# Six blocks of idle F32R matmuls of 192 and 384 columns behind the last product of a convolution and feed-forward kernel

## The chip, the cores and the metric

The kernel runs on one core of one Trainium2 chip. Its time is device microseconds of one execution, here the median of three runs. A separate execution was taken with the hardware profiler; its trace is what is read below.

## The reference

```python
def _attn_ref(x, weight):                      # x: 8 x 4096 x 192, weight: 8 heads x 7 taps
    w = softmax(weight, axis=-1)
    x_pad = np.concatenate([np.zeros((B, K - 1, D)), x], axis=1)
    x_unf = x_pad[:, idx, :].reshape(B, S, K, H, group)
    return np.einsum('hk,bskhg->bshg', w, x_unf).reshape(B, S, D)

def _moe_ref(x, w_in, w_out):                  # 32768 tokens, 192 -> 2048 -> 192
    h = x @ w_in
    g = np.where(h >= 1, h, np.where(h <= -1, 0.0, (h + 1) ** 2 / 4))
    return (g @ w_out).astype(np.float32)
```

The output of the first function, taken as 32768 tokens of 192 channels, is the input of the second. All is float32.

## The kernel before, in words

The tokens are worked off in 64 blocks of 512 (`TB`), the 2048 inner channels in eight pairs of 128 (`NPAIR`), so that the main loop has 512 steps `q`. Per step TensorE (PE) multiplies the tokens by a part of `w_in` (`mm1`, line 528) into the PSUM tile `h`, ScalarE and VectorE make `g` of it, and two or three steps later `mm2` (line 586) multiplies `g` by a part of `w_out` and adds into four PSUM tiles, `accm0`, `accm1`, `accr0` and `accr1`, until a block of tokens is done. To keep float32 accuracy with matmuls of the faster type F32R, the operands are split into a rounded part (`hi`) and the rest (`lo`), each of type F32R, and three of the four cross products are summed. The split `w_in` stays in SBUF for the whole kernel in eight tiles `W`, each of 128 partitions, two parts and 384 columns. The contraction length of 192 is 128 + 64 rows, so most matmuls take one half of PE's array (64 rows, `HALVES`), and two of them, one on each half, run as a pair. In the early steps plain F32 matmuls are used instead (lines 510, 513, 528, and 553 of `mm2_first`); one F32 product appears in the trace as two matmul instructions, each with a weight load of its own.

The order of the instructions is written out by hand (`manual_schedule`): each engine runs its own instructions in the order in which the program issues them, and waits for another engine only by semaphores.

The end is of its own. `evac_last` (lines 710 to 716) reads the four accumulators of the last block out to SBUF before the last pair of inner channels is added. `pair_last` then forms the last pair's product for each of four groups of 128 tokens in F32, 192 columns on the whole array (`units`, line 733), transposes the sums read out before (`others`, lines 737 and 738), adds both on VectorE (`total`, line 742) and stores the result (line 743). Groups 0 and 1 use tiles of `h`; groups 2 and 3 use new tiles with the names `accm0`, `accm1`, `accr0` and `accr1`. A new tile of such a name takes the place of the one before, and its first writer waits until the old one has been read.

At the start of the kernel the function `idle_matmuls` (line 786) issues seven bf16 matmuls whose results nothing reads.

Of the kernel before, what the change touches and what calls it, by code (L numbers as in the profile page):

```python
# [8 lines left out]
F32 = mybir.dt.float32  # L9
# [9 lines left out]
P = 128  # L19
TB = 512  # L20
# [13 lines left out]
def lightconv_then_ffn(ctx: ExitStack, tc: tile.TileContext, x, weight, w_in, w_out, out):  # L34
# [24 lines left out]
    nc = tc.nc  # L59
    B, S, D = x.shape  # L60
# [7 lines left out]
    NPAIR = NF // 2  # L68
# [3 lines left out]
    HALVES = (TOP, BOT)  # L72
# [10 lines left out]
    ps_o = ctx.enter_context(tc.tile_pool(name="ps_o", bufs=1, space=PSUM))  # L83
# [273 lines left out]
    W = [const.tile([P, 2, CI], F32R, name=f"w{j}") for j in range(NPAIR)]  # L357
# [177 lines left out]
    def tokens_of(t, b, turned):  # L535

        if not turned:
            return t[:, b * P:(b + 1) * P]
        return t.rearrange("p (k i a) -> p k a i", k=2, a=2)[:, b % 2, b // 2]
# [179 lines left out]
    def pair_last(q):  # L719

        s = q // NPAIR
        g, w = gs.pop(q), WF[NPAIR - 1 + LAG]
        y = [ob.tile([P, TB], F32, name="sum") for _ in range(2)]
        y = [y[b // 2][:, b % 2 * D:(b % 2 + 1) * D] for b in range(4)]
        h = [ps_h.tile([P, 2, TB], F32, name="h") for _ in range(2)]
        a = [ps_o.tile([P, TB], F32, name=n) for n in ("accm0", "accm1", "accr0", "accr1")]
        ps = [t[:, 0:D] for t in (h[0][:, 0], h[1][:, 0], a[0], a[1])]
        ot = [t[:, 0:D] for t in (h[0][:, 1], h[1][:, 1], a[2], a[3])]
        part = lambda a, b: last[a][:, b * P:(b + 1) * P]

        def units(b):
            for e in range(2):
                nc.tensor.matmul(ps[b], tokens_of(g[:, e], b, True), w[:, e, :],  # L733
                                 start=(e == 0), stop=(e == 1))

        def others(b):
            nc.tensor.matmul(ot[b][:, P:], part("r", b), ident[:, 0:DR], start=True, stop=True)  # L737
            nc.tensor.transpose(ot[b][:, 0:P], part("m", b), plain)
            nc.scalar.copy(y[b], ot[b])

        def total(b):
            nc.vector.tensor_tensor(out=y[b], in0=ps[b], in1=y[b], op=ALU.add)
            (nc.scalar if b == 2 else nc.sync).dma_start(
                out=out[s * TB + b * P:s * TB + (b + 1) * P], in_=y[b])

        units(0)
        units(1)
        others(0)
        others(1)
        total(0)  # L750
        total(1)
        units(2)
        others(2)
        others(3)
        units(3)
        total(2)
        total(3)


    whose = const.tile([P, 2 * P], F32, name="whose")  # L760
# [300 lines left out]
    for q in range(NQ + LATE):  # L1061
        s, j = divmod(q, NPAIR)
        c, i = divmod(q, 2 * NPAIR)
# [53 lines left out]
        else:  # L1117
# [12 lines left out]
            n = q - 1 if q < NF32 + 3 else q - 2  # L1130
# [66 lines left out]
```

## Time and profile before

| | |
|---|---|
| median of 3 runs | 2021.41 us (2021.04 to 2021.7) |
| the profiled execution | 2020.79 us |
| its span, first to last instruction | 2019.1 us |
| PE busy | 2014.9 us, 18659 matmuls |
| ScalarE, VectorE, GpSimd busy | 1955.8, 1873.3, 790.3 us |
| start of PE's last matmul, VectorE's last addition, the last store's issue | 2015.48, 2015.91, 2016.30 us |
| mean granted clock of PE | 1.000 |

Times inside the trace are microseconds from the start of the span. PE's matmuls are pipelined and the end of one is modelled, so the record of one is longer than the distance to the next one; what a matmul costs in a row of matmuls is read from the distances of their starts. PEld are the weight loads, which PE runs beside the matmuls. Line 1193 is the end of the program, where all engines meet.

### The profile page before, as it was taken

How to read it: one execution, taken by the hardware profiler on the slowest of the kernel's cores; microseconds unless marked ns; L12 is line 12 of the kernel's file. 1: busy time of each engine (PE TensorE's matmuls, PEld its weight loads, DVE VectorE, ACT ScalarE, POOL GpSimd, SP SyncE). 2: the span in 40 equal slices, each digit the busy share in tenths (PEclk: the TensorE clock that was granted, in tenths of full speed). 3: DMA queues.
4: the chain of work that ended last, by engine and by line, in shares of the span. 5: the costliest groups of instructions: out<-in, count | busy, mean ns of one | idle time of the engine just before them, and what ended most of it. 6: DMA issues, size and time to landing. Idle time of an engine off the chain costs nothing.

```text
span 2019.1 us, 46948 instructions
## 1 busy us (share of the span) xinstructions
PE 2014.9 (100%) x18659; PEld 1747.2 (87%) x18659; DVE 1873.3 (93%) x2109; ACT 1955.8 (97%) x2376; POOL 790.3 (39%) x762
## 2 busy tenths in 40 slices
PE   9999999999999999999999999999999999999999
PEld 7988888888888888888888888888888888888888
DVE  8899999999999999999999999999999999999988
ACT  8899999999999999999999999999999999999997
POOL 3534434343444343434433334344433343443340
PEclk9999999999999999999999999999999999999999
DMA  7334334443443434344434444344343434443332
GB/s 191 82 67 77 61 75 76 78 77 68 75 78 68 80 68 76 72 78 79 73 62 75 77 77 78 66 74 79 67 80 68 78 72 78 75 75 64 74 62 48
DMA packets 470909, 152.79 MB, mean 76 GB/s; under 512 B 419056, under 2 KB 426544, under 8 KB 470688
## 3 DMA queue, kind: packets, MB, share of 16 engines
q1 hardware_dynamic: 447008, 109.50, 26.9%
q0 software_dynamic: 23520, 40.19, 12.9%
q8 instruction: 146, 2.39, 0.5%
q14 instruction: 75, 0.61, 0.1%
q10 hardware_dynamic: 160, 0.10, 0.0%
HBM read 32.84 MB, written 25.17 MB: 29 GB/s over the span
## 4 chain that ended last, share of the span: by engine, by line
PE 100%; POOL 0%; DVE 0%; issue 0%; DVEq 0%
PE h L528 49%; PE accr L586 32%; PE accm L586 16%; PE accm L553 1%; PE accr L553 1%; PE accm L786 0%; PE accr L219 0%; PE accm L197 0%; PE h L733 0%; PE accm L733 0%; PE accr L513 0%; PE accr L510 0%; PE accm L510 0%; POOL t L778 0%; PE h L175 0%; PE h L737 0%
## 5 line engine op out<-in xcount | busy, mean ns | idle before, releaser
L639 DVE TENSOR_TENSOR gl<-g,gh 128x1024 fp32r<-128x1024 f32 x495 | 639.1, 1291 | 94.2 <-ACT gh L633 94.1
L968 DVE SCALAR_TENSOR_TENSOR g<-g,h 128x1024 f32<-128x1024 f32 (+1 forms) x506 | 608.8, 1203 | 9.4 <-ACT g L621 5.4
L528 PE MATMUL h<-hi,w 64*128 64x512 f32 x4048 | 602.1, 377 | 0.0
L586 PE MATMUL accr<-gh,wg 64*128 64x512 f32 x3960 | 587.6, 376 | 0.0
L621 ACT ACTIVATE g<-g 128x1024 f32<-128x1024 f32 x499 | 528.2, 1058 | 15.9
L620 ACT ACTIVATE g<-h 128x1024 f32<-128x1024 f32 x499 | 509.1, 1020 | 24.8 <-PE h L528 20.5
L633 ACT CAST gh<-g 128x1024 fp32r<-128x1024 f32 x495 | 513.8, 1038 | 1.2 <-DVE g L968 1.1
L528 PEld LDWEIGHTS h<-hi,w 64*128 64x128 f32 x4048 | 379.5, 186 | 56.5
L586 PEld LDWEIGHTS accr<-gh,wg 64*128 64x128 f32 x3960 | 370.8, 185 | 56.6
L270 POOL TENSOR_TENSOR y<-y,p 128x512 f32<-128x512 f32 x181 | 233.3, 1289 | 403.4 <-DVE m L645 289.3
L270 POOL TENSOR_TENSOR r<-r,p 128x512 f32<-128x512 f32 x180 | 231.6, 1287 | 402.1 <-DVE m L645 399.3
L528 PE MATMUL h<-lo,w 64*128 64x512 f32 x2024 | 382.2, 376 | 0.0
L586 PE MATMUL accr<-gl,words 64*128 64x512 f32 x1980 | 373.9, 376 | 0.0
L645 DVE TENSOR_TENSOR m<-gl 128x512 fp32r<-128x512 f32 x495 | 340.4, 688 | 27.2 <-DVE gl L639 0.9
L528 PE MATMUL h<-rh,w 64*128 64x512 f32 x1000 | 294.7, 376 | 0.0
L586 PE MATMUL accm<-gh,wg 64*128 64x512 f32 x1980 | 293.8, 376 | 0.0
L528 PE MATMUL h<-rhi,w 64*128 64x512 f32 x992 | 293.6, 376 | 0.0
L676 POOL DMA_DIRECT2D t<-t x244 | 206.8, 981 | 31.6 <-ACT t L666 23.2
L528 PEld LDWEIGHTS h<-lo,w 64*128 64x128 f32 x2024 | 189.9, 186 | 28.5
L586 PEld LDWEIGHTS accr<-gl,words 64*128 64x128 f32 x1980 | 185.8, 186 | 27.9
L586 PEld LDWEIGHTS accm<-gh,wg 64*128 64x128 f32 x1980 | 185.8, 186 | 27.9
L301 POOL TENSOR_TENSOR lo<-y,hi 128x512 fp32r<-128x512 f32 x62 | 79.9, 1289 | 316.5 <-ACT p L261 166.3
(170 smaller groups left out, 2379.6 us busy)
## 6 DMA issues: line engine op xcount, KB each, us to landing
t<-t POOLq DMA_DIRECT2D x183, 128.0 KB, 3.9
out_dram<-osb SPq DMA_DIRECT2D x366, 64.0 KB, 1.9
raw<-in_x_dram SPq DMA_DIRECT2D x334, 68.0 KB, 2.4
hi<-hi SPq DMA_DIRECT2D x130, 128.0 KB, 2.3
lo<-lo SPq DMA_DIRECT2D x128, 128.0 KB, 3.5
t<-t POOLq DMA_DIRECT2D x61, 256.0 KB, 3.2
rhi<-rh SPq DMA_DIRECT2D x62, 128.0 KB, 2.2
rlo<-rl SPq DMA_DIRECT2D x62, 128.0 KB, 3.5
```

The lines of the kernel that those rows point to most:

```text
L270: fresh.append(lambda p=self.product(k): nc.gpsimd.tensor_add(y, y, p))
L301: sub = eng.tensor_sub(lo, self.y, hi.bitcast(F32))
L528: nc.tensor.matmul(h[e], w[HALVES[e], c0:c0 + P], seen(x[e][e]), start=(n == 0), stop=(n == len(mms) - 1))
L553: nc.tensor.matmul(accs[s][a, i][:, c0:c0 + D], block, w[half, e, :], start=(j == 0 and e == 0 and b % 2 == 0), stop=(j == NPAIR - 1 and e ...
L586: mm = nc.tensor.matmul(accs[s][bank], w[half], in_turn(g[half]), start=(j == 0 and bank not in seen), stop=(j == NPAIR - 1 and k % 3 == 2 ...
L620: nc.scalar.activation(g[:, e, :], hs[q][:, e, :], AF.Relu, bias=0.5, scale=0.5)
L621: nc.scalar.activation(g[:, e, :], g[:, e, :], AF.Square)
L633: nc.scalar.copy(gh[:, e, :], gs[q][:, e, :])
L639: nc.vector.tensor_sub(gl[:, e, :], g[:, e, :], gh[:, e, :])
L645: return nc.vector.tensor_add(gt, gl[:, 0, :], gl[:, 1, :])
L676: nc.gpsimd.dma_start(out=to, in_=src, accum_op=ALU.add)
L968: nc.vector.scalar_tensor_tensor(out=g, in0=g, scalar=1.0, in1=h, op0=ALU.min, op1=ALU.max)
```

## The change

Behind the last call of `total`, `pair_last` calls a new function, `idle_blocks`. It takes four new PSUM tiles with the accumulators' names, of which it writes two, and issues six blocks of F32R matmuls. Weights and moving columns both come from the eight tiles `W` (both parts, 16 in all, one after another); `D` is 192, `P` is 128. Every matmul starts and ends its own sum, and nothing reads the results. In the sixth block the weights change only with every third matmul.

```diff
         total(2)
         total(3)
+        idle_blocks()
+
+    def idle_blocks():
+
+        t = [ps_o.tile([P, TB], F32, name=n) for n in ("accm0", "accm1", "accr0", "accr1")]
+        w = lambda i, n, half=slice(0, P): W[i % NPAIR][half, i // NPAIR % 2, 0:n]
+        for i in range(24):
+            nc.tensor.matmul(t[i % 2][:, 0:D], w(i, P), w(i + 11, D), start=True, stop=True)
+        for i in range(24):
+            for k, half in enumerate(HALVES):
+                nc.tensor.matmul(t[k][:, 0:D], w(i, P, half), w(i + 11, D, half),
+                                 start=True, stop=True)
+        for i in range(16):
+            nc.tensor.matmul(t[i % 2][:, 0:2 * D], w(i, P), w(i + 11, 2 * D),
+                             start=True, stop=True)
+        for i in range(16):
+            nc.tensor.matmul(t[i % 2][:, 0:D if i % 2 else 2 * D], w(i, P),
+                             w(i + 11, D if i % 2 else 2 * D), start=True, stop=True)
+        for i in range(16):
+            for k, half in enumerate(HALVES):
+                nc.tensor.matmul(t[k][:, 0:2 * D], w(i, P, half), w(i + 11, 2 * D, half),
+                                 start=True, stop=True)
+        for i in range(24):
+            nc.tensor.matmul(t[i % 2][:, 0:D], w(i // 3, P), w(i + 11, D), start=True, stop=True)
```

The order of PE's instructions changes at one place, its end. The first listing is the difference there: a row is a line, the operation, the tile written, the tiles read (the moving one first, then the weights) and the shape written; buffer numbers stand behind the names.

```order
 L733 MATMUL accm_30158<-wf_109,g_30079 128x192 x2
-L1193 UNCONDITIONAL_BRANCH
+L765 MATMUL accm_30189<-w_89,w_86 128x192
+L765 MATMUL accm_30190<-w_90,w_87 128x192
+L765 MATMUL accm_30189<-w_91,w_88 128x192
+L765 MATMUL accm_30190<-w_92,w_89 128x192
```

Where PE's program ended with the last product, the new matmuls follow; the branch to the end stands behind all 160 of them. The second listing is the same place of the changed kernel with full tile names and with what an instruction waits for.

```order
L738 MATMUL accr1_30160<-osb_29929,t_30139 128x128
L733 MATMUL accm1_30158<-wf9_109,g_30079 128x192 x2
L765 MATMUL accm0_30189<-w3_89,w0_86 128x192 [waits DVE_49]
L765 MATMUL accm1_30190<-w4_90,w1_87 128x192 [waits DVE_49]
L765 MATMUL accm0_30189<-w5_91,w2_88 128x192
L765 MATMUL accm1_30190<-w6_92,w3_89 128x192
```

Only the first two new matmuls wait, each for VectorE, which reads the `accm` tiles of the groups 2 and 3 before; no instruction of another engine is added, and none waits for the new matmuls but the program's end.

## Rows read from the trace of the kernel before

**Rows 1.** The page: its span, its part 1 for PE, its part 4.
```profile
span 2019.1 us, 46948 instructions
...
PE 2014.9 (100%) x18659; PEld 1747.2 (87%) x18659; DVE 1873.3 (93%) x2109; ACT 1955.8 (97%) x2376; POOL 790.3 (39%) x762
...
PE 100%; POOL 0%; DVE 0%; issue 0%; DVEq 0%
```

**Rows 2.** The time line from 2015 us: start, us, engine, line, instruction, count [idle before <-releaser].
```profile
2015.25 0.36 DVE L742 TENSOR_TENSOR sum<-accm,sum 128x192 f32<-128x192 f32 x1 [0.32 <-ACT sum L739]
...
2015.48 0.33 PE L733 MATMUL accm<-wf,g 128*128 128x192 f32 x1
...
2015.91 0.36 DVE L742 TENSOR_TENSOR sum<-accm,sum 128x192 f32<-128x192 f32 x1 [0.31 <-PE accm L733]
2016.30 0.33 SPq L743 DMA_DIRECT2D out_dram<-sum  x1
```

**Rows 3.** Line L1193, the end: count, shortest/median/longest in ns, first and last start.
```profile
L1193 POOLq EVENT_SEMAPHORE  x4: 17/17/17, 2018.3 to 2019.0; - x4
...
L1193 SPq DRAIN  x3: 7/7/7, 2018.2 to 2018.5; - x3
L1193 PEldq DRAIN  x2: 13/900/1788, 2014.1 to 2018.6; - x2
```

**Rows 4.** Stretches: busy us of PE, PEld, DVE, ACT, POOL, granted clock, DMA share, GB/s.
```profile
2015.80:2018.30 2.50, 0.01 (x1) 0.00 (x0) 0.36 (x1) 0.00 (x0) 0.00 (x0) 1.00 0.38 127
2018.30:2019.10 0.80, 0.00 (x0) 0.00 (x0) 0.00 (x0) 0.00 (x0) 0.00 (x0) 0.50 0.00 0
```

**Rows 5.** The time line from 2012.6 us: a read-out and the weight load behind it.
```profile
2012.66 0.37 ACT L716 COPY t<-accr 64x256 f32<-64x256 f32 x1 [0.50 <-DVE t L714]
2013.08 0.19 PEld L737 LDWEIGHTS h<-ident,t 128*128 128x128 f32 x1
```

**Rows 6.** The chain in order of time at 1005 us: start, us, what.
```profile
1005.54 1.94 PE h L528 x18
1007.48 0.65 PE accr L586 x6
```

**Rows 7.** The time line from 2013.2 us, L737 and L738.
```profile
2013.47 0.33 PE L737 MATMUL h<-ident,t 128*128 128x64 f32 x2
...
2013.53 0.20 PEld L738 LDWEIGHTS h<-osb,t 128*128 128x128 f32 x1
...
2013.64 0.28 PE L738 MATMUL h<-osb,t 128*128 128x128 f32 x1
```

**Rows 8.** The same time line, L733 and what follows it.
```profile
2013.64 0.65 PEld L733 LDWEIGHTS accm<-wf,g 128*128 128x128 f32 x4
2013.76 0.82 PE L733 MATMUL accm<-wf,g 128*128 128x192 f32 x4
...
2014.41 0.33 PE L737 MATMUL accr<-ident,t 128*128 128x64 f32 x2
```

**Rows 9.** The time line from 11.5 us, weight loads of L513 on the two halves.
```profile
11.71 0.18 PEld L513 LDWEIGHTS accr<-rh,p 64*128 64x128 f32 x1 [0.33 <-issue]
11.71 0.18 PEld L513 LDWEIGHTS accm<-rh,p 64*128 64x128 f32 x1
11.81 0.19 PEld L513 LDWEIGHTS accr<-rh,p 64*128 64x128 f32 x1
11.82 0.19 PEld L513 LDWEIGHTS accm<-rh,p 64*128 64x128 f32 x1
```

**Rows 10.** Groups by line, engine and shape: xcount | busy us, mean ns | idle before.
```profile
L786 PE MATMUL accm<-osb 128*128 128x512 bf16 x5 | 2.3, 629 | 0.0
```

**Rows 11.** The time line from 18 us, F32 matmuls of 192 columns on halves.
```profile
18.47 0.82 PE L553 MATMUL accr<-wf,g 64*128 64x192 f32 x8
...
19.12 0.82 PE L553 MATMUL accm<-wf,g 64*128 64x192 f32 x8
```

## The prediction

> **What bounds the kernel now.** I read the page first: TensorE (PE) is busy for the whole span of 2019.1 us and the chain that ended last is PE on nearly every step [rows 1]. So there is nothing ahead of the end to gain or lose; the change touches only what lies behind the last product. There the time line is the view to read [rows 2]. The last matmul of L733 starts at 2015.48 and its record ends at 2015.81; VectorE's last addition (L742) follows at 2015.91 for 0.36, SyncE issues the last store at 2016.30, and then no engine computes any more. The rows of line L1193, the program's end, show what closes it [rows 3]: PE's own drain begins at 2014.1, lasts 1.788 and so ends at 2015.9, just behind the last matmul. SyncE, which waits for the store, gets to its drain at 2018.2 to 2018.3, and from there a round of semaphores over all engines runs to 2019.1. PE is one of those that must arrive. From 2015.8 to 2018.3 it could therefore work for nothing, 2.5 us; each microsecond past 2018.3 is paid in full. The granted clock is 1.00 (2.4 GHz) up to 2018.3 and 0.50 behind it [rows 4]: PE had then been idle for 2.5 us. In the changed kernel PE resumes within 0.6 us, so I count everything at 2.4 GHz.
>
> **The change part by part.** It removes and moves nothing. It adds 160 matmuls (24 + 48 + 16 + 16 + 32 + 24), each with a weight load, in 120 slots (a pair on the halves is one), on PE alone, behind PE's last product: block 1, 24 on the whole array with 192 columns; block 2, 24 pairs on the halves with 192; block 3, 16 whole with 384; block 4, 16 whole that alternate 384 and 192; block 5, 16 pairs on the halves with 384; block 6, 24 whole with 192 where three in a row load the same weights. No other engine gets an instruction, no DMA is added, and nothing reads the results.
>
> *When it starts.* The first matmul writes accm0, which L742 has read by 2015.25 + 0.36 = 2015.61; it runs while PE would wait anyway and is not counted. The second writes accm1, which the last L742 reads until 2015.91 + 0.36 = 2016.27. From an engine's end to PE's load I take 0.05: L716 ended at 2012.66 + 0.37 = 2013.03 and the load that waited for it started at 2013.08 [rows 5]. A load with nothing to hide it takes 0.11 (below). So the second matmul runs from 2016.27 + 0.05 + 0.11 = 2016.43. SyncE's store was issued without PE and lies beside all this, hidden.
>
> *What a column costs.* All steady matmuls here are of the same type as the added ones (F32R), on halves, with 512 columns: 18 of them, nine pairs, in 1.94 us [rows 6], 0.2156 per pair, which is one column per cycle. The two halves of a pair run together. Scaled by columns, 384 cost 0.162 and 192 cost 0.081. For 384 this is nearly certain.
>
> *What a short matmul costs* is the open price: no row of the trace shows an F32R matmul below 512 columns, nor one on the whole array. Its load is fetched while the matmul before runs, so a slot is the longer of moving time and load time. From below: 0.081, the moving time alone, if the load is as short as that of the second pass of L737, which started 0.06 after the first, its load included (the pair begins at 2013.47, and the load of L738, which is issued as the second pass begins, at 2013.53) [rows 7]. Nearest to it: the load of L738 began at 2013.53 and its matmul at 2013.64, 0.11 later, although the matmul before it has only 64 columns. L738 is, like an added matmul, one instruction with one load of 128 columns of 4-byte weights; L737 is an F32 product in two passes with a load each. So I take **0.110 per 192-column slot**, bound by its load. From above: F32 products of 192 columns on the whole array (L733), four passes from 2013.76 to 2014.41 [rows 8]: 0.1625 a pass, two passes or 0.325 a product. For a pair on the halves I take the same 0.110: at L513 the loads of both halves were issued at 11.71 and the next two at 11.81 and 11.82 [rows 9], so they load side by side in 0.11. Repeated weights I count as loaded again, since every matmul of the trace has its own load.
>
> *The sum.* Block 1: 24 x 0.110 = 2.64. Block 2: 24 x 0.110 = 2.64. Block 3: 16 x 0.162 = 2.59. Block 4: eight times 0.162 (a 384, which hides the next load) + 0.110 = 2.18. Block 5: 2.59. Block 6: 2.64. Together 15.28, less the first matmul 15.17. Between whole array and halves there are four changes (blocks 1 to 2, 2 to 3, 4 to 5, 5 to 6). No row shows such a change without a wait in it; each costs nothing at least, and at most an emptied array: 0.17 by which the record of an L733 matmul (0.33) outlasts its slot, and 0.11 for an uncovered load, together 0.28. I take half, 0.14 each, 0.56.
>
> End: 2016.43 + 15.17 + 0.56 = 2032.16; the last record's tail 0.17, the drain some 0.05, the round of semaphores 2019.1 - 2018.3 = 0.8, and the span ends at 2033.18. That is 14.1 more than 2019.1. The profiled execution took 2020.79; with 14.1 it is 2034.9. It stands 0.6 below the median of the runs (2021.41), so I name **2035.5**.
>
> The Trainium skill ("TensorEngine Tiling (Array Packing)", Key Properties) says that changing the tiling mode drains TensorE. By that the changes would stand at the upper end, 1.12 in place of 0.56, and the time at 2036.1; no run here shows it yet.
>
> **The rivals.**
> *One column per cycle everywhere.* If the load hides even under 192 columns, block 1, 2 and 6 cost 1.94 each and block 4 costs 1.94: 12.95 in all, 2.3 less, **2033.2**. For it: the short loads of L737's second passes. Against it: L738.
> *Short F32R runs like F32.* If a matmul of 192 columns gets the F32 price of L733, 0.325, blocks 1, 2 and 6 cost 7.80 each and block 4 8 x (0.162 + 0.325) = 3.90: 32.48, 17.0 more, **2052.5**. For it: the fast pace is shown at 512 columns only, and operands are 4-byte in both. Against it: it is one instruction, F32 is two. Half of this (one pass at two cycles per column, 0.1625) gives 19.48 and **2039.6**.
> *Loads in line with matmuls.* If on the whole array the next load waits for the matmul to end, a 192 costs 0.081 + 0.110 = 0.191 and a 384 0.272: 4.58 + 2.64 + 4.35 + 3.70 + 2.59 + 4.58 = 22.44, 7.1 more, **2042.6**. Against it: L733's four loads stand inside its matmuls (from 2013.64 and 2013.76), with 0.1625 a slot, the time of the moving columns alone [rows 8]. The Trainium skill ("TensorE: Matmul & The Clock Gate", Part 3, The mechanism) says that a load overlaps running matmuls only if its row group differs, which would be this case; the trace disagrees with its 0.1625.
> *Not slower.* The matmuls don't reach the chip, or cost so little that they end before 2018.3: nothing reads their results, and a build may drop such work. The point that decides: 120 slots would have to fit into 2018.3 - 2016.43, 16 ns each, or be gone. Then **2021.4**. Against it: the idle matmuls of L786 are never read either and stand in the trace [rows 10], and the added ones stand in PE's order.
> *Fed too slowly.* On the halves, 192 columns in 0.110 ask for four instructions in that time, 27 ns each. At L553 sixteen instructions (eight matmuls, eight loads) take 0.65, 41 ns each [rows 11]; if that were PE's limit, block 2 would cost 24 x 0.163 = 3.90, 1.3 more: 2036.8.
>
> **How the numbers follow.** My forecast 0.37; one column per cycle everywhere 0.21; like F32 0.25; half of that 0.08; loads in line 0.04; not slower 0.02; 0.03 for the slow feeding and what I don't name. The forecast's own range is 2034.6 to 2036.8. The low end of the range is the rival at 0.081 without the 0.56 for the changes, 2032.6, and 0.3 for the spread of the runs; leaving out the F32 pace would leave out over 2 in 10, so the high end is that case with 1.12 for the changes, 2053.1. A measurement of this kernel can tell 0.2%, 4 us; every case but one is slower by over 10 us: slower 0.97, same 0.02, faster 0.01.
>
> **What would show it.** In the profile after: nothing changed up to 2015.8; PE resumes at about 2016.4; blocks 1 and 6 equal at 2.6 each, block 3 and 5 equal at 2.6, block 2 like block 1; granted clock 1.00 until PE's end; the span ends 0.8 to 0.9 behind PE. Block 1 at 1.9 shows the hidden load, at 3.9 or 7.8 a slower moving pace; block 6 shorter than block 1 shows that repeated weights cost less. A start later than 2016.5, or a clock of 0.50 inside the blocks, makes the sum wrong elsewhere.

## The result and the profile after

The changed kernel took 2036.11 us, median of 3 runs (2035.91 to 2036.52), against 2021.41 before: a ratio of 1.0073 with a 95% interval of 1.005 to 1.0096, slower by 14.7 us or 0.7%. The forecast was 2035.5. The profiled execution took 2035.91 with a span of 2034.2 (before 2020.79 and 2019.1 [rows 1]), so the span grew by 15.1 where 14.1 was worked out.

The page of the changed kernel: PE runs through, 160 matmuls more than before.

```profile
span 2034.2 us, 47268 instructions
...
PE 2032.1 (100%) x18819; PEld 2003.4 (98%) x18819; DVE 1872.8 (92%) x2109; ACT 1957.6 (96%) x2376; POOL 790.4 (39%) x762
```

The time line of the weight loads from 2016 us on, the place that answers to [rows 2]. One row is one block: start, length, line, shape of the weights, number of loads, and the idle time of the load queue before it. A load of 128 columns has a record of 0.19, so the distance of loads in a row is its length less 0.19, over the number less one.

```profile
2016.48 2.64 PEld L765 LDWEIGHTS accm<-w,w 128*128 128x128 f32 x23 [0.48 <-DVE sum L742]
2019.23 2.75 PEld L768 LDWEIGHTS accm<-w,w 64*128 64x128 f32 x48
2022.09 2.75 PEld L771 LDWEIGHTS accm<-w,w 128*128 128x128 f32 x16
2024.83 2.35 PEld L774 LDWEIGHTS accm<-w,w 128*128 128x128 f32 x16
2027.35 2.75 PEld L778 LDWEIGHTS accm<-w,w 64*128 64x128 f32 x32 [0.16 <-issue]
2030.35 0.86 PEld L781 LDWEIGHTS accm<-w,w 128*128 128x128 f32 x7 [0.25 <-issue]
...
2032.58 0.53 PEld L781 LDWEIGHTS accm<-w,w 128*128 128x128 f32 x4
```

The first of 24 is missing in the row of L765: it ran at 2015.82, while PE would wait anyway, and the second waited for VectorE's last addition, as forecast. Block 1 is (2.64 - 0.19) / 22 = 0.111 a slot, and the starts of its matmuls give 0.1115 as well. Block 2 has 24 pairs in the same 0.1115 (the two loads of a pair are 3 to 4 ns apart). Block 6 has 0.1115 too: its weights repeat in threes, and each of its 24 matmuls still has its own load. Blocks 3 and 5 have 0.175 a slot on average, by the starts of their matmuls: the first slots are uneven (0.174 to 0.185), then both settle at 0.1735. Block 4 has 0.284 for a 384 and a 192 together.

Two close-ups of the time line show what binds: first three matmuls of block 1 with their loads, then three of block 3.

```profile
2017.80 0.50 PE L765 MATMUL accm<-w,w 128*128 128x192 f32 x3
2017.82 0.41 PEld L765 LDWEIGHTS accm<-w,w 128*128 128x128 f32 x3
...
2024.14 0.68 PE L771 MATMUL accm<-w,w 128*128 128x384 f32 x3
2024.14 0.53 PEld L771 LDWEIGHTS accm<-w,w 128*128 128x128 f32 x3
```

In block 3 each load begins as the matmul before begins, and loads that bind come every 0.1115, so that in a slot of 0.1735 the load has room to spare: the columns set the slot. In block 1 the load begins 0.02 behind the matmul, because it has to wait for the load before it, and the loads come evenly every 111 or 112 ns while the matmuls come at 109 to 117: the load sets the slot.

The end, in the rows of the program's last line (L1217 here, the L1193 of [rows 3]; count, shortest/median/longest in ns, first and last start), PE's last row of the time line, and the stretch behind PE (columns as in [rows 4]):

```profile
L1217 SPq EVENT_SEMAPHORE  x11: 17/28/14994, 2016.8 to 2034.1; - x11
...
L1217 SPq DRAIN  x3: 7/7/7, 2033.4 to 2033.7; - x3
...
L1217 PEldq DRAIN  x2: 13/1106/2200, 2031.1 to 2033.7; - x2
```

```profile
2032.67 0.61 PE L781 MATMUL accm<-w,w 128*128 128x192 f32 x4
```

```profile
2033.35:2034.20 0.85, 0.00 (x0) 0.00 (x0) 0.00 (x0) 0.00 (x0) 0.00 (x0) 1.00 0.00 0
```

PE's last record ends at 2033.28, its drain at 2031.1 + 2.2 = 2033.3. SyncE now waits 14.994 for PE, from 2018.3 to 2033.3, and the span ends 0.9 behind it. The granted clock was 1.00 (2.4 GHz) in every stretch from 2015.8 to the end.

Three things were left to explain: why the short slot is 0.1115 (the rivals had 0.081, 0.1625, 0.191 and 0.325), why the 384-column slot is 0.175 and not the 0.162 that I had called nearly certain, and what the changes between whole array and halves cost.

### The profile page after: what moved, and what is told of

Same layout as the page of the kernel before. It is cut to its first block, busy times and chain, and to the rows that moved or that the text cites. A ratio compares the mean times of both kernels' runs of the same rounds, so it can differ in the third digit from the quotient of the medians.

```text
span 2034.2 us, 47268 instructions
## 1 busy us (share of the span) xinstructions
PE 2032.1 (100%) x18819; PEld 2003.4 (98%) x18819; DVE 1872.8 (92%) x2109; ACT 1957.6 (96%) x2376; POOL 790.4 (39%) x762
## 4 chain that ended last, share of the span: by engine, by line
PE 100%; POOL 0%; DVE 0%; issue 0%; DVEq 0%
PE h L528 49%; PE accr L586 32%; PE accm L586 16%; PE accm L553 1%; PE accr L553 1%; PE accm L778 0%; PE accm L771 0%; PE accm L810 0%; PE accm L768 0%; PE accm L781 0%; PE accm L765 0%; PE accr L219 0%; PE accm L774 0%; PE accm L197 0%; PE h L733 0%; PE accm L733 0%
## 5 line engine op out<-in xcount | busy, mean ns | idle before, releaser
L528 PE MATMUL h<-hi,w 64*128 64x512 f32 x4048 | 662.6, 377 | 0.0
L586 PE MATMUL accr<-gh,wg 64*128 64x512 f32 x3960 | 652.7, 376 | 0.0
L528 PEld LDWEIGHTS h<-hi,w 64*128 64x128 f32 x4048 | 474.1, 186 | 0.3
L528 PE MATMUL h<-lo,w 64*128 64x512 f32 x2024 | 449.1, 376 | 0.0
L586 PEld LDWEIGHTS accr<-gh,wg 64*128 64x128 f32 x3960 | 432.5, 185 | 13.5
L586 PE MATMUL accr<-gl,words 64*128 64x512 f32 x1980 | 439.1, 376 | 0.0
L586 PE MATMUL accm<-gh,wg 64*128 64x512 f32 x1980 | 326.4, 376 | 0.0
L528 PE MATMUL h<-rh,w 64*128 64x512 f32 x1000 | 294.7, 376 | 0.0
L528 PE MATMUL h<-rhi,w 64*128 64x512 f32 x992 | 293.5, 376 | 0.0
L528 PEld LDWEIGHTS h<-lo,w 64*128 64x128 f32 x2024 | 256.8, 186 | 0.1
L586 PEld LDWEIGHTS accr<-gl,words 64*128 64x128 f32 x1980 | 251.0, 186 | 0.0
L586 PEld LDWEIGHTS accm<-gh,wg 64*128 64x128 f32 x1980 | 232.3, 186 | 0.0
L586 PE MATMUL accm<-m,words 64*128 64x512 f32 x990 | 219.5, 376 | 0.0
```

Of the source, the lines that this page charges most:

```text
L528: nc.tensor.matmul(h[e], w[HALVES[e], c0:c0 + P], seen(x[e][e]), start=(n == 0), stop=(n == len(mms) - 1))
L586: mm = nc.tensor.matmul(accs[s][bank], w[half], in_turn(g[half]), start=(j == 0 and bank not in seen), stop=(j == NPAIR - 1 and k % 3 == 2 ...
```

## The experiments

All of them replace or edit `idle_blocks` alone. Where no median is named, a time is that of one execution. Distances are those of the starts of matmuls in a row, at a granted clock of 1.00 unless another is named.

### What sets the short slot

**Other lengths.** Four blocks of 24 on the whole array, with 64, 128, 256 and 320 columns.

```diff
-            nc.tensor.matmul(t[i % 2][:, 0:D], w(i, P), w(i + 11, D), start=True, stop=True)
+            nc.tensor.matmul(t[i % 2][:, 0:64], w(i, P), w(i + 11, 64), start=True, stop=True)
...
```

> Four blocks of 24 whole-array matmuls with changing weights and 64, 128, 256 and 320 columns in place of the six. Theory A, a slot is the longer of the weight load (0.1115 us) and the moving columns: 0.11 at 64 and at 128 columns, about 0.118 at 256, 0.145 at 320. Rival B, a fixed price and a price per column, as a line through 0.1115 at 192 and 0.1735 at 384: 0.070, 0.091, 0.132, 0.153. Rival C, short matmuls run at two cycles per column: 0.056, 0.109 and above 0.118 at 256.

Measured: 2034.58, span 2032.9. The time line of the loads of the 64-column block and of the first 128-column slots, and the stretches:

```profile
2016.98 2.64 PEld L765 LDWEIGHTS accm<-w,w 128*128 128x128 f32 x23 [0.48 <-DVE sum L742]
...
2019.87 1.42 PEld L767 LDWEIGHTS accm<-w,w 128*128 128x128 f32 x12
```

```profile
2017.00:2019.50 2.50, 2.50 (x23) 2.50 (x23) 0.00 (x0) 0.00 (x0) 0.00 (x0) 1.00 0.35 116
2019.55:2021.40 1.85, 1.85 (x19) 1.85 (x18) 0.00 (x0) 0.00 (x0) 0.00 (x0) 1.00 0.00 0
2021.50:2022.80 1.30, 1.30 (x8) 1.30 (x8) 0.00 (x0) 0.00 (x0) 0.00 (x0) 0.50 0.00 0
2023.00:2028.00 5.00, 5.00 (x25) 5.00 (x25) 0.00 (x0) 0.00 (x0) 0.00 (x0) 0.50 0.00 0
2028.30:2031.60 3.30, 3.30 (x24) 3.30 (x24) 0.00 (x0) 0.00 (x0) 0.00 (x0) 1.00 0.00 0
```

64 columns take the same 2.64 for 23 loads as 192 do: 0.1115, and 128 columns the same. Theory A stands; every price that falls with the columns is out. The granted clock, which none of the theories had expected to move, fell to 0.50 (1.2 GHz) at 2021.45 in the middle of the 128-column block and came back at 2028.28. Under it a slot took 0.2135, at 128 and at 256 columns alike, so that the 256-column block says nothing of 2.4 GHz. The 320-column block behind it ran at 1.00 with 0.147.

**Narrower weights.** 24 matmuls each with weights of 64, 64 and 32 columns, and 192, 64 and 64 moving columns.

```diff
-            nc.tensor.matmul(t[i % 2][:, 0:D], w(i, P), w(i + 11, D), start=True, stop=True)
+            nc.tensor.matmul(t[i % 2][0:64, 0:D], w(i, 64), w(i + 11, D), start=True, stop=True)
...
```

> Three blocks of 24: weights of 64 columns with 192 moving columns, weights of 64 with 64 moving, weights of 32 with 64 moving. Theory A, the load binds and goes by the columns of the weights: the first block is bound by the moving columns, 0.081 to 0.092 us a slot, the second 0.056, the third 0.03 to 0.06. Rival, the load takes the same time whatever it loads, or the slot is set by something else: 0.11 in all three.

Measured: 2023.92, span 2022.2. The loads of the three blocks:

```profile
2016.86 2.05 PEld L765 LDWEIGHTS accm<-w,w 128*64 128x64 f32 x23 [0.53 <-DVE sum L742]
2018.87 1.50 PEld L767 LDWEIGHTS accm<-w,w 128*64 128x64 f32 x24
2020.29 0.85 PEld L769 LDWEIGHTS accm<-w,w 128*32 128x32 f32 x24
```

With half the weights the 192 columns take 0.089, no longer 0.1115; with 64 moving columns the slot is 0.058, and 0.032 with 32 columns of weights. In the last case 64 moving columns alone would take 0.027 at one column per cycle, so 0.032 is only an upper bound for the load. The load's price goes by the columns of the weights, 0.1115 for 128 and 0.058 for 64, and the slot is the longer of load and moving columns. Both sides of that are now shown.

**The F32 pace.** Products of plain F32 with 192, 64 and 16 columns, to see what a pass of L733 and L737 costs [rows 7, 8].

```diff
+        f = lambda i, n: w(i, n).bitcast(F32)
...
-            nc.tensor.matmul(t[i % 2][:, 0:D], w(i, P), w(i + 11, D), start=True, stop=True)
+            nc.tensor.matmul(t[i % 2][:, 0:D], f(i, P), f(i + 11, D), start=True, stop=True)
...
```

> Blocks of 16 F32 products (two matmul instructions each) with 192, 64 and 16 columns, weights of 128 columns that change. Theory 1, each pass of an F32 product loads half of what an F32R matmul loads, as the 0.06 of L737's second pass suggests: 0.325 us a product, then 0.112 to 0.116, then 0.11. Theory 2, each pass loads like F32R: 0.325, 0.223, 0.223. Theory 3, the first pass loads like F32R, the second in half of it: 0.325, 0.167, 0.167.

Measured: 2031.53, span 2029.8.

```profile
2021.51 3.70 PEld L768 LDWEIGHTS accm<-w,w 128*128 128x128 f32 x32
2025.14 3.65 PEld L770 LDWEIGHTS accm<-w,w 128*128 128x128 f32 x32
```

A pass of 192 columns takes 0.1625, as at L733. 64 columns and 16 columns both take 0.1115 a pass, two passes a product: each pass waits for a load of its own. Theory 2 stands. The second pass of L737 had looked as if its load took 0.06. Here, too, the second matmul of the 64-column block starts 0.056 behind the first, and from then on they come every 0.1115: the record of a matmul can start while its own load is still running, so one distance of starts says nothing of the load. My lower bound of 0.081 rested on that reading.

**One half alone.** 16 matmuls of 384 columns on the whole array (read in the order of the next section), then 24 of 192 columns on the upper half alone.

```diff
-            for k, half in enumerate(HALVES):
-                nc.tensor.matmul(t[k][:, 0:D], w(i, P, half), w(i + 11, D, half),
-                                 start=True, stop=True)
...
+            nc.tensor.matmul(t[2 + i % 2][:, 0:D], w(i, P, TOP), in_turn(w(i + 11, D, TOP)),
+                             start=True, stop=True)
```

> 16 whole-array matmuls of 384 turned columns, then 24 of 192 turned columns on the upper half alone. Theory, the load of one half binds as that of the whole array: 0.1115 us a matmul at a granted clock of 1.00, so a pair on both halves gives twice the matmuls in the same time. Rival, a half's load takes half as long, and a pair's two loads stand one behind the other: 0.081 to 0.09 a matmul, bound by its columns.

Measured: 2025.31, span 2023.6.

```profile
2019.76 2.75 PEld L768 LDWEIGHTS accr<-w,w 64*128 64x128 f32 x24 [0.23 <-issue]
```

24 loads of 64 rows take 2.75, as the 48 of block 2 did: 0.1115 each. Half the rows make a load no shorter, and a pair loads both halves at once. Pairs on the halves do two matmuls in the time of one.

### Why 384 columns took more than scaled

**The order of the columns.** The steady matmuls from which I scaled (L528, L586) read their moving columns in turns, one from each half of the row (`in_turn`, "p (a b) -> p b a"). The idle blocks read them one after another. The run has seven blocks of 16 on the whole array: 384 in turn, 384 straight, 384 straight from other tiles (`WG`), 512 in turn and straight, 256 in turn and straight.

```diff
+        flat = lambda ts, i, n: ts[i % NPAIR].rearrange("p a b -> p (a b)")[:, 0:n]
...
+            nc.tensor.matmul(t[i % 2][:, 0:384], w(i, P), in_turn(flat(W, i + 3, 384)),
...
+            nc.tensor.matmul(t[i % 2][:, 0:384], w(i, P), flat(W, i + 3, 384), start=True, stop=True)
...
```

> Seven blocks of 16 on the whole array, all with changing weights from W: 384 columns of W in the turned order of the kernel's own steps, 384 of W one after another (block 3 of the change), 384 of WG one after another, 512 of W turned, 512 of W one after another, 256 turned, 256 one after another. Theory O, columns that are read one after another cost the 11 ns that block 3 had over the price per column: 0.162 us a slot, 0.1735, 0.1735, 0.2156, 0.227 to 0.23, 0.1115 (load), 0.118. Rival S, weights and columns from the same tiles get in each other's way: 0.1735 for both orders, 0.162 with WG. Rival N, every matmul on the whole array costs it: 0.1735 in the first three, 0.227 in both with 512.

Measured: 2038.19, span 2036.5.

```profile
2016.45 2.41 PEld L767 LDWEIGHTS accm<-w,w 128*128 128x128 f32 x15 [0.48 <-DVE sum L742]
2018.84 2.80 PEld L770 LDWEIGHTS accm<-w,w 128*128 128x128 f32 x16
2021.63 2.79 PEld L772 LDWEIGHTS accm<-wg,w 128*128 128x128 f32 x16
2024.40 3.38 PEld L774 LDWEIGHTS accm<-w,w 128*128 128x128 f32 x16
2027.81 3.63 PEld L776 LDWEIGHTS accm<-w,w 128*128 128x128 f32 x16
2031.48 1.98 PEld L778 LDWEIGHTS accm<-w,w 128*128 128x128 f32 x16
2033.37 1.98 PEld L781 LDWEIGHTS accm<-w,w 128*128 128x128 f32 x16
```

By the starts of the matmuls (a row of loads mixes its first slot with the block before): 384 in turn 0.1625, straight 0.1735, straight from `WG` 0.1733; 512 in turn 0.2157, straight 0.2265; 256 in turn 0.1115, the load's own price, and straight 0.120. The straight order costs 0.011 a matmul, at 384 and at 512 alike, so it is no price per column, and another tile does not take it away. Theory O stands, N falls, and S falls for these 0.011. Two things stay open. The first slots of a straight block read from `W` are uneven before they settle, six of them between 0.168 and 0.185 at 384 columns and nine between 0.224 and 0.239 at 512; from `WG`, or in turn, they are even from the start. So a small part of S may hold, 0.002 a slot on average at 384. And why the order matters isn't shown. It seems to depend on the load as well: with weights of 64 columns 192 straight columns took 0.089 (the run with narrower weights), 0.009 over one column per cycle at 2.4 GHz, where 256 to 512 straight columns with weights of 128 stand 0.013 over it. No other order than these two was tried.

**The change in the turned order.** The same six blocks, each moving operand wrapped.

```diff
-            nc.tensor.matmul(t[i % 2][:, 0:2 * D], w(i, P), w(i + 11, 2 * D),
+            nc.tensor.matmul(t[i % 2][:, 0:2 * D], w(i, P), in_turn(w(i + 11, 2 * D)),
...
```

> The six blocks of the change, with all moving columns in the turned order. Theory, 384-column slots are bound by their columns and lose the price of the order: blocks 3 and 5 fall from 0.1735 and 0.170 to 0.1625 us a slot, two slots of block 4 from 0.284 to 0.274, and blocks 1, 2 and 6, bound by their loads, stay at 0.1115; the end comes 0.35 to 0.45 us sooner after PE's last product than with the change. Rival, the order matters to every block or to none: blocks 1, 2 and 6 shorten as well (0.2 us each for 9 ns a slot), or blocks 3 and 5 stay.

Measured: 2036.01 median of 4 (2035.34 to 2036.34), ratio 1.0075 (1.0058 to 1.0092) to before; span of the profiled execution 2033.6.

```profile
2016.44 2.64 PEld L765 LDWEIGHTS accm<-w,w 128*128 128x128 f32 x23 [0.48 <-DVE sum L742]
2019.18 2.75 PEld L768 LDWEIGHTS accm<-w,w 64*128 64x128 f32 x48
2022.03 2.57 PEld L771 LDWEIGHTS accm<-w,w 128*128 128x128 f32 x16
...
2026.99 2.57 PEld L778 LDWEIGHTS accm<-w,w 64*128 64x128 f32 x32
```

Blocks 3 and 5 lose 0.18 each against the rows above (2.57 for 2.75), at 0.1625 a slot; block 4 has 0.274 for a 384 and a 192; the load-bound blocks 1, 2 and 6 stay at 0.1115, so the theory stands. The uneven first slots are gone too. (Block 5 had stood at 0.1735 like block 3, pair to pair; the 0.170 of the expectation is the distance from the second matmul of a pair to the next pair.) From the start of PE's last product (2015.60) to the end of PE's last record (2032.71) it is 17.11, against 2015.64 and 2033.28, 17.64, in the changed kernel: 0.53 less, a little more than the 0.35 to 0.45 expected. The medians lie 0.1 apart, and single runs of this kernel 1.0; against before on the same chip (2021.11) it is even 14.9 slower, where the change was 14.7. Half a microsecond is read in the trace here, not in the times.

### What a change between whole array and halves costs

12 times one whole-array matmul and one pair on the halves, 192 columns each, then 24 on the upper half.

```diff
-        for i in range(24):
-            nc.tensor.matmul(t[i % 2][:, 0:D], w(i, P), w(i + 11, D), start=True, stop=True)
-        for i in range(24):
+        for i in range(12):
+            nc.tensor.matmul(t[0][:, 0:D], w(i, P), w(i + 11, D), start=True, stop=True)
...
```

> First block: 12 times one whole-array matmul and one pair on the halves, 192 columns, 24 slots with 23 changes between whole array and halves. Theory: each change costs the 0.2 us that block boundaries cost in the change, so 24 x 0.1115 + 23 x 0.2 = 7.3 us. Rival, the 0.2 belong to the start of a new block, not to the change of the array's use: 24 x 0.1115 = 2.7 us. Second block: 24 matmuls on the upper half alone. Theory, the load binds there as well: 0.1115 a matmul, as long as a whole pair.

Measured: 2032.01, span 2030.3. A piece of PE's time line, and the stretches:

```profile
2018.32 0.35 PE L765 MATMUL accm<-w,w 128*128 128x192 f32 x1
2018.61 0.36 PE L767 MATMUL accm<-w,w 64*128 64x192 f32 x2
2018.89 0.35 PE L765 MATMUL accm<-w,w 128*128 128x192 f32 x1
...
2019.47 0.35 PE L765 MATMUL accm<-w,w 128*128 128x192 f32 x1
```

```profile
2016.50:2022.30 5.80, 5.78 (x30) 3.71 (x29) 0.34 (x1) 0.00 (x0) 0.00 (x0) 1.00 0.15 51
2022.35:2024.00 1.65, 1.65 (x8) 1.14 (x7) 0.00 (x0) 0.00 (x0) 0.00 (x0) 0.50 0.00 0
2024.05:2028.90 4.85, 4.85 (x25) 4.85 (x24) 0.00 (x0) 0.00 (x0) 0.00 (x0) 0.50 0.00 0
```

The whole-array matmul returns every 0.573. Two slots of 0.1115 are 0.223 of it; the two changes make the other 0.350, 0.175 each. The theory stands, with 0.175 for its 0.2, and the rival falls. In the changed kernel the four boundaries come to the same: from the start of a block's last matmul to that of the next block's second, less the two slots between, 0.18, 0.20, 0.175 and 0.18. Between blocks 3 and 4, both on the whole array, the step is 0.174, a plain slot: a new block by itself costs nothing. At a change the next load no longer runs beside the matmul before it. Here are the last pair of block 5 and the first loads of block 6 in the changed kernel:

```profile
2030.08 0.34 PE L778 MATMUL accm<-w,w 64*128 64x384 f32 x2
2030.35 0.52 PEld L781 LDWEIGHTS accm<-w,w 128*128 128x128 f32 x4 [0.25 <-issue]
```

The load begins 0.27 behind the matmul (0.18 to 0.21 at the other three changes), where inside a block, from its second matmul on, it begins 0.00 to 0.03 behind. The clock fell to 0.50 at 2022.33 in the run of this section; the upper half alone then took 0.2135 a matmul, where 192 columns at 1.2 GHz would be 0.160: the load binds at either level and takes twice the time at half the clock.

### The two ends of the sum

**No wait at the start.** The blocks write two tiles of `h` that have long been read, in place of the accumulators' tiles.

```diff
-        t = [ps_o.tile([P, TB], F32, name=n) for n in ("accm0", "accm1", "accr0", "accr1")]
+        t = [ps_h.tile([P, 2, TB], F32, name="h")[:, 0] for _ in range(2)]
```

> The six blocks unchanged, but written into tiles of h, whose readers are done by 2015.0, instead of accm0 and accm1. Theory: the blocks start 0.8 us earlier, as soon as PE's last product has been issued, and the span is 0.8 us shorter than with the change, each block as long as before. Rival, the start is not set by the readers of the tiles: no difference to the change, 14.7 us over the kernel before.

Measured: 2035.34 median of 4 (2035.23 to 2035.6), before on the same chip 2021.33, ratio 1.007 (1.0054 to 1.0085); span 2033.6.

```profile
2015.22 0.82 PE L733 MATMUL accm<-wf,g 128*128 128x192 f32 x4
...
2015.75 2.96 PE L765 MATMUL h<-w,w 128*128 128x192 f32 x24
```

The blocks start right behind the last product. From that product's start (2015.72) to PE's end it is 16.95 in place of 17.64: 0.68 less and not the 0.8 expected: the wait of 0.8 is gone, but so is the hiding place of the first matmul, 0.11. What PE does not wait for, it ends earlier by.

**Work that fits into the shadow.** Twelve matmuls of block 1 alone.

```diff
-        for i in range(24):
+        for i in range(12):
             nc.tensor.matmul(t[i % 2][:, 0:D], w(i, P), w(i + 11, D), start=True, stop=True)
...
```

> Only the first 12 matmuls of block 1. Theory, PE is free until the last store has landed: the twelfth ends at 2018.0, before SyncE reaches its drain at 2018.3, so the time is that of the kernel before, within 0.4 us, and the span is equal. Rival, work behind the last product adds its own length: 12 x 0.1115 = 1.3 us more.

Measured: 2021.06 median of 11, before 2021.33 median of 15, ratio 0.9999 (0.999 to 1.0008); span 2019.3.

```profile
2016.55 1.48 PE L765 MATMUL accm<-w,w 128*128 128x192 f32 x11 [0.31 <-DVE sum L742]
```

The row of SyncE in the program's last line, here L1201:

```profile
L1201 SPq DRAIN  x3: 7/7/7, 2018.5 to 2018.8; - x3
```

PE ends at 2018.03, before SyncE, which waits for the last store, gets to its drain at 2018.5, and the twelve cost nothing. The shadow behind PE's last product, read from [rows 3], is real.

## Right or wrong, step by step

**Right: the place and the start.** Nothing is paid for the work until the store has landed (the run with twelve), PE's end sets the span's end past it, and the second idle matmul starts where VectorE's last addition lets it: 2016.57 by the matmuls behind it, against 2016.43. The 0.14 is no error of the step: PE's last product itself started at 2015.64 in this execution, 0.16 later than in [rows 2].

**Right: the short slot, and its reason.** 0.110 was taken as the price of a load; 0.1115 was measured in the blocks 1, 2 and 6, for 64 and 128 columns too, and it fell only with the columns of the weights. Over 71 slots (23, 24 and 24) the 0.0015 is 0.11. That pairs load side by side and that repeated weights are loaded again held as well. Part of this was luck: the 0.110 from L738 and the 0.06 from L737 were witnesses of one kind, single distances of starts, and the F32 run shows that such a distance need not be the load's price.

**Wrong in size: "384 cost 0.162", "nearly certain".** The step scaled a row of matmuls by their columns, and did not ask whether the new ones read their columns as those did. They take 0.1753 on average in blocks 3 and 5 (16 x 0.0133 = 0.21 more in each) and 0.284 for 0.272 in block 4 (8 x 0.012 = 0.10 more): 0.52 in all. The order of the moving columns is the cause of nearly all of it: in turn, blocks 3 and 5 run at 0.1625 and block 4 at 0.274, and the uneven first slots are gone. Of the 0.0133 a slot, the settled slots of 0.1735 make 0.0115 and the uneven first ones the rest. That the order is the cause is shown; by what means stays open.

**Wrong in size: four changes at 0.14.** 0.175 to 0.20 was measured, 0.74 for 0.56, inside the bounds of 0 and 0.28. The Trainium skill ("TensorEngine Tiling (Array Packing)", Key Properties) had it that a change of mode drains the engine. The runs agree that each change costs something, 0.175 in a row of them, and the late loads at the changes would fit a drain; the 1.12 that I had put under that rule, 0.28 a change, is half as much again as the 0.74 measured.

**The sum.** 0.14 at the start, 0.11 for short slots, 0.52 for the 384 columns and 0.18 for the changes make 0.95; the tail, the drain and the round of semaphores (2033.11 to 2034.2 is 1.09, forecast 1.02) give the other 0.07. Together 1.02: the span of 2034.2 against 2033.18. That the median came out only 0.6 above the forecast is chance: the profiled execution of before lay 0.6 below its median, that of after 0.2.

**The rivals.** *One column per cycle everywhere* fell: its witness, the second pass of L737, was a matmul that starts within its own load. *Short F32R like F32*, on which I had put 0.25, fell with 0.1115 against 0.325 (F32 measured beside it); the fast pace does not need 512 columns, it is only hidden behind the load below some 256. *Loads in line* fell: the close-ups show each load beginning at most 0.02 behind the matmul before it, on the same rows. The Trainium skill ("TensorE: Matmul & The Clock Gate", Part 3, The mechanism) lets a load overlap matmuls in flight only if its row group differs; these runs, like L733, disagree, with 0.1735 for 384 columns on the whole array, where load and columns in line would take over 0.27. The same section also lets a load go ahead if it is for a background weight buffer; these runs would fit that, but none shows such a buffer. *Fed too slowly* fell: block 2 fed four instructions in 0.1115, 28 ns each. *Not slower* fell with the result.

## What to carry to other kernels

Cost a row of short F32R matmuls by the load of its weights, here 0.11 at a granted clock of 1.00 for 128 columns of weights, of 64 or 128 rows and however few columns move: join moving columns up to about 256, run pairs on the halves, or narrow the weights, and keep matmuls on the halves together, since each change to or from the whole array costs about 0.18. Before a price is scaled from another row, compare how the two read their operands, not only type and shape. Behind the last product there is a shadow as long as the last addition and the last store take (2.5 here): what ends inside it is free, what ends later is paid in full.

## What was not expected of the hardware

- Moving columns read in turns from two halves of a row cost 0.011 less a matmul than columns read one after another, at 384 and 512 columns (0.1625 and 0.1735, 0.2157 and 0.2265).
- A matmul's record can start before its own load has ended: 0.056 behind the one before it, at the head of a block whose loads take 0.1115 each.
- The granted clock fell to 0.50 although PE was busy without a gap: at 2021.45 after 64- and 128-column slots that were mostly load, at 2022.33 in the run that alternated whole array and halves. It came back at 2028.28 in the first of the two, after 256-column slots at 1.2 GHz. In the changed kernel, whose blocks 1 and 2 are load-bound as well but move 192 columns in each slot, it stayed at 1.00. So it did in the F32 run, whose passes of 64 and then 16 columns are load-bound too (the row below). What of the activity decides this was not tried.

```profile
2021.70:2028.70 7.00, 7.00 (x65) 7.00 (x64) 0.00 (x0) 0.00 (x0) 0.00 (x0) 1.00 0.00 0
```

- The load follows that clock: 0.1115 at 1.00, 0.2135 at 0.50.
